# One emformer attention + ReGLU kernel: a new load order in the head, other block sizes, and a re-timed planner

## The chip, the cores and the metric

The kernel runs on one NeuronCore of a Trainium2 chip. The metric is the device time of one execution in microseconds (us). The core has a matrix engine (TensorE, PE in the profile, with its weight loads as PEld), a vector engine (VectorE, DVE), a scalar engine (ScalarE, ACT), GpSimd (POOL, which here mostly issues loads) and SyncE (SP, which here issues transfers). All transfers run on 16 DMA engines that these share.

## The reference

Two stages follow each other. The first is chunked attention: 4 batches, 8 heads, 768 positions, head size 64. Each chunk of 32 queries sees 8 memory keys, 16 keys to its left, its own 32 and 8 to its right.

```python
k_full = np.concatenate([mem_k, k_ctx], axis=2)
v_full = np.concatenate([mem_v, v_ctx], axis=2)
scores = scale * np.matmul(q_c, k_full.transpose(0, 1, 3, 2))
scores = scores - np.max(scores, axis=-1, keepdims=True)
a = np.exp(scores)
a = a / (np.sum(a, axis=-1, keepdims=True) + 1e-09)
out[:, :, c_start:c_end] = np.matmul(a, v_full)
```

The second is a gated feed-forward layer on the 3072 rows that result (512 wide, 1536 hidden):

```python
gate = np.maximum(x @ w_gate, 0.0)
val = x @ w_val
return (gate * val @ w_out).astype(np.float32)
```

## The kernel before

**Tiles and blocks.** The 3072 rows are 24 tiles of 128 rows, six to a batch. Attention runs tile by tile: `scores` (L297), `row_max` (L315), `subtract` (L325), `exponent` (L334), `row_sum` (L340), `reciprocal`, `normalise` (L348), a transposition of P, `values` (L369), and `x_copy` (L392), which puts the tile's attention output, already transposed, into a block's `xT`. The feed-forward layer runs block by block: a block is 2 to 4 consecutive tiles (`BLOCKS`, L51). `first` (L402) multiplies all of a block's columns by 128 hidden units of a gate or value weight, four matmuls to a group; `relu` (L411) on ACT and `gate` (L416) on DVE make the hidden activations; `second` (L428) makes the output rows and `store` (L436) copies and writes them. A block's `first` needs all of its tiles' `x_copy`. Blocks 0 and 1 (tiles 0 to 3) are interleaved by four weight groups (`GROUPS`: hidden pieces 0-1, 2-5, 6-8, 9-11), as the weights arrive.

**Batch 0 and the rest.** For tiles 0 to 5, q and k are loaded in pairs of tiles (`load_pair`, L226) and transposed on PE with an identity (`pair_t`, L234); ACT or DVE copies the result out of PSUM (`pair_copy`, L240). v of batch 0 is loaded in its natural layout (`load_v_tile`, L196) and shifted to the chunks' contexts on PE (`shift`, L205) and copied (`shift_copy`). For later tiles, q and k are loaded tile by tile (`load_qk`), and v of a batch is loaded straight into `v_bd`. From tile `LATE_QK` on, a transposing DMA issued by SP does the q and k transposition (`qk_transfer`, L281) in place of PE (`qk_t`, L275), and one copy of the keys remains; the scores read the queries where the DMA put them. From tile `LATE_P` on, SP also transposes P (`p_transfer`, L361) in place of PE and a copy (`p_t`, `p_copy`).

**Order of the work.** All instructions are emitted by a planner written in the kernel (`schedule`, L692). Each operation has the engines that may run it with planned durations, its dependencies, a priority, and buffers that it takes and gives back. The planner steps through planned time, gives each free engine its first ready operation by priority (attention of a tile comes before feed-forward work), and appends it to that engine's program. The engines then execute those programs in order, each waiting where its next operation's data are not there yet. So a planned duration moves no instruction by itself; it changes the order. Planned landings of loads are in L746-750; those of the SP transfers in L779-781 with `LAND` and `LAND_P` (L518-519) added. Until a planned 18 us (`WARM`), PE is given products on zeros (`idle_product`) wherever it has nothing ready.

**Queues.** POOL issues the loads in the order of the calls from L644 on. SP issues the small memory-value rows of batch 1 and the transposing DMAs. The load of v for batch 2 waits until `v_bd[0]` is cleared, which is planned after `("tc", 12, 1)`, the key copy of tile 12; the load of v for batch 3 waits for `hold` (L684), planned after the values of tile 11 and the key copy of tile 17. Loads of q and k of tile 16 and later stand behind v of batch 2 in POOL's order.

Of the kernel before, what the change touches and what calls it, by code (L numbers as in the profile page):

```python
# [19 lines left out]
def kernel(  # L20
# [29 lines left out]
    NSET = 2  # L50
    BLOCKS = [2, 2, 2, 4, 4, 4, 4, 2]  # L51
    GROUPS = [(0, 2), (2, 6), (6, 9), (9, 12)]
    BAND0 = 48
    UT = 3

    LATE_QK, LATE_P = 11, 10

# [459 lines left out]
    ISSUE, SLACK = 1.5, 1.0  # L517
    LAND = {a: 4.0 if a < 16 else 3.5 if a < 19 else 2.0 for a in range(NT)}  # L518
    LAND_P = {a: 3.0 if a < 14 else 2.5 if a < 18 else 2.0 for a in range(NT)}

# [3 lines left out]
    for a in range(NT):  # L524
        b, t = divmod(a, TPB)
        last = t == TPB - 1
        for i in (1, 0):
            if b == 0:
                if t % 2 == 0:
                    for j in range(2):  # L530
                        op(("t", a + j, i), {"PE": 0.3}, lambda e, a=a, i=i, j=j: pair_t(a // 2, i, j),
                           [("pl", a // 2, i), "ib", ("new", b)], (1, a - i, -2 + j), ["aps"], ["qk"] * j)
                        op(("tc", a + j, i), psum16(HP * 128) if t else {("ACT", "DVE")[j]: psum16(HP * 128)[("ACT", "DVE")[j]]}, lambda e, a=a, i=i, j=j: pair_copy(a // 2, i, j, engine[e]),
                           [("t", a + j, i)], (1, a - i, -2 + j), (), ["aps"])
# [125 lines left out]
    for par in range(2):  # L660
        load(("vm", par), 256, 0.3, lambda par=par: mem_values(par))
    for a, i in late[:5]:
        load_qk_op(a, i)
    for i in range(2):
        load(("wo", i), 768, 4.1, lambda i=i: load_out(i))
    for b in range(1, B):
        deps = ([("z0", hp, c0) for hp in range(HP) for c0 in range(0, NCH, 8)] if b > 1 else [("z1", hp) for hp in range(HP)]) + ([("v", TPB * (b - NSET + 1) - 1)] + ['hold'] if b > NSET else [])
        if b == 1:
            for n in range(2 * HP):
                op(("mr", b, n), {"SP": 0.72}, lambda e, b=b, n=n: mem_rows(nc.sync, b, n),  # L670
                   deps + [(("vm", 0), 0.2), (("vm", 1), 0.2)], (0,))
        for par in range(2):
            load_v_op(b, par, deps)
        if b == 2:
            for n in range(2 * HP):
                load(("mr", 2, n), 192, 0.22, lambda n=n: mem_rows(nc.gpsimd, 2, n),
                     deps + [(("vm", 0), 0.2), (("vm", 1), 0.2)])
        for a, i in late[(5, 20, 26)[b - 1]:(20, 26, 36)[b - 1]]:
            load_qk_op(a, i)
    for n in range(2 * HP):  # L680
        load(("mr", 3, n), 192, 0.22, lambda n=n: mem_rows(nc.gpsimd, 3, n),
             deps + [(("vm", 0), 0.2), (("vm", 1), 0.2)])

# [8 lines left out]
    def schedule():  # L692
        done, started, times = {}, set(), [0.7]
        free = {e: 0.7 for e in ("PE", "ACT", "DVE", "SP", "POOL")}
        queue_end, flying, gives = 0.0, [], [(WARM + 0.15, "fps")]
        room["fps"] -= 1
# [27 lines left out]
        while len(started) < len(ops) + len(loads):  # L724
# [8 lines left out]
            while moved:  # L733
                moved = False
                for e in ("POOL", "PE", "ACT", "DVE", "SP"):
                    if free[e] > t + 1e-9:
                        continue
                    if e == "POOL":
# [98 lines left out]
```

## Time and profile before

| what | value |
|---|---|
| median of 3 runs (lowest, highest) | 241.21 us (241.03, 241.58) |
| the profiled execution's own time | 240.65 us |
| its span, first to last instruction | 238.9 us |
| PE busy, of the span | 232.5 us, 97% |
| DVE, ACT, POOL busy | 145.3, 135.5, 77.4 us |
| mean granted TensorE clock | 0.998 of full speed |
| first feed-forward product starts | 22.89 us |
| last PE work ends | 235.1 us |

Times in the profile are microseconds from the start of the span. A row of the timeline gives start, length from first start to last end, engine, the kernel's line, operation, what it writes and reads, the shapes, how many instructions are merged in it, and in brackets how long the engine stood idle before and what ended that. Matmul ends are modelled and overlap with the next start, so that the time a group really takes is read from start to start.

### The profile page before, as it was taken

To read this page: it belongs to the slowest core of one execution; us is meant where nothing else is said; L and a number is where in the kernel's file an instruction comes from. 1 tells how busy PE (TensorE), PEld (TensorE's weight loads), DVE (VectorE), ACT (ScalarE), POOL (GpSimd) and SP (SyncE) were. 2 spreads that over 40 slices of the span, in tenths; PEclk is the share of its full clock that TensorE was granted. 3 is DMA by queue.
4 is the path that set the end of the run, shared out by engine and by line. 5 is a ranking of instruction groups with operands and counts; after the bars stand their busy time and mean duration, and the time that the engine had idled before them with its cause. 6 is when DMAs were issued, how large, how long until landed. Compare 5 with 4: busy or idle time off the path is not lost.

```text
span 238.9 us, 6437 instructions
## 1 busy us (share of the span) xinstructions
PE 232.5 (97%) x2654; PEld 137.7 (58%) x2654; DVE 145.3 (61%) x292; ACT 135.5 (57%) x284; POOL 77.4 (32%) x102
## 2 busy tenths in 40 slices
PE   7898999999999999999999999999999999999994
PEld 5577887785589644455544444444555444445873
DVE  6674876987888389994279851599960043410430
ACT  7577777866885456897566851365523233312422
POOL 8975779313920374700094552100000000000000
PEclk9999999999999999999999999999999999999999
DMA  6999999999999999996199999995121300012102
GB/s 74 171 179 202 201 166 161 206 133 125 190 166 138 131 156 118 122 129 136 70 141 101 135 154 91 113 209 64 27 43 47 127 4 0 0 47 88 44 3 88
DMA packets 103069, 26.88 MB, mean 113 GB/s; under 512 B 94080, under 2 KB 99968, under 8 KB 103040
## 3 DMA queue, kind: packets, MB, share of 16 engines
q0 software_dynamic: 76128, 14.65, 92.7%
q1 hardware_dynamic: 23312, 5.53, 23.2%
q10 hardware_dynamic: 3600, 6.29, 8.4%
q8 instruction: 21, 0.34, 0.7%
q14 instruction: 8, 0.07, 0.2%
HBM read 28.55 MB, written 6.29 MB: 146 GB/s over the span
## 4 chain that ended last, share of the span: by engine, by line
PE 93%; DMA 2%; POOL 2%; issue 1%; ACT 1%; ACTq 0%; POOLq 0%
PE v_ps L408 27%; PE g_ps L408 26%; PE out_ps L433 26%; PE xT_ps L389 3%; PE s_ps L310 2%; DMA v_n<-in_v_dram 2%; PE idle_ps L140 2%; PE vs_ps L216 2%; PE xT_ps L382 2%; PE qk_ps L279 1%; PE pT_ps L359 1%; POOL qk_p L229 1%; PE qk_ps L238 1%; PE xT_ps L375 1%; POOL v_n L200 0%
## 5 line engine op out<-in xcount | busy, mean ns | idle before, releaser
L420 DVE TENSOR_TENSOR gvT<-v_ps,g_relu 128x256 f16<-128x256 f32 (+1 forms) x96 | 53.0, 554 | 48.7 <-PE v_ps L408 35.1
L408 PE MATMUL v_ps<-xT,w_val_sb 128*128 128x256 f16 (+1 forms) x384 | 78.2, 326 | 0.1
L408 PE MATMUL g_ps<-xT,w_gate_sb 128*128 128x256 f16 (+1 forms) x384 | 78.1, 326 | 0.0
L414 ACT ACTIVATE g_relu<-g_ps 128x256 f16<-128x256 f32 (+1 forms) x96 | 47.0, 490 | 41.5 <-PE g_ps L408 39.8
L433 PE MATMUL out_ps<-w_out_sb,gvT 128*128 128x512 f16 (+2 forms) x300 | 65.8, 371 | 0.0
L408 PEld LDWEIGHTS <-w_gate_sb 128*128 128x128 f16 x384 | 36.9, 98 | 24.8
L408 PEld LDWEIGHTS <-w_val_sb 128*128 128x128 f16 x384 | 35.9, 98 | 22.5 <-issue 0.5
L433 PEld LDWEIGHTS <-gvT 128*128 128x128 f16 x300 | 27.6, 97 | 29.5
L79 ACT COPY o_sb<-out_ps 128x512 f32<-128x512 f32 (+2 forms) x25 | 14.2, 568 | 29.6 <-PE out_ps L433 19.4
L323 DVE TENSOR_REDUCE mx<-s_ps 128x8 f32<-128x512 f32 x24 | 16.4, 685 | 13.9 <-PE s_ps L310 13.5
L338 ACT ACTIVATE p_exp<-dif 128x256 f16<-128x256 f32 (+2 forms) x72 | 19.6, 339 | 6.3 <-DVE dif L330 6.1
L184 POOL DMA_DIRECT2D v_bd<-in_v_dram x12 | 11.0, 924 | 33.6 <-DVE v_bd L684 19.2
L342 DVE TENSOR_REDUCE sm<-p_exp 128x8 f32<-128x512 f16 x24 | 16.4, 683 | 5.0 <-ACT p_exp L338 4.8
L257 POOL DMA_DIRECT2D qk_b<-in_k_dram x18 | 16.2, 902 | 9.7 <-DMA v_bd<-in_v_dram 5.4
L257 POOL DMA_DIRECT2D qk_b<-in_q_dram x18 | 16.2, 899 | 9.7 <-DMA v_bd<-in_v_dram 7.2
L79 ACT COPY v_bd<-v_bd 24x768 f16<-24x768 f16 (+1 forms) x23 | 18.5, 823 | 1.2 <-ACT o_sb L79 0.9
L353 DVE TENSOR_TENSOR p_n<-p_exp,rinv 128x512 f16<-128x512 f16 x24 | 16.5, 686 | 0.3
L330 DVE TENSOR_TENSOR dif<-s_ps,mx 128x512 f32<-128x512 f32 x24 | 16.2, 674 | 0.2
L79 ACT CAST xT<-xT_ps 128x512 f16<-128x512 f32 x17 | 10.0, 586 | 8.5 <-PE xT_ps L389 7.3
L167 POOL DMA_DIRECT2D v_bd<-vmem x16 | 10.2, 645 | 12.4 <-DMA qk_b<-in_q_dram 6.1
L140 PE MATMUL idle_ps<-idle 128*128 128x256 bf16 x69 | 11.3, 314 | 1.1 <-DVE warm L477 1.1
L389 PEld LDWEIGHTS <-v_bd 128*128 128x128 f16 x288 | 9.8, 96 | 3.6
(60 smaller groups left out, 165.6 us busy)
## 6 DMA issues: line engine op xcount, KB each, us to landing
out_dram<-o_sb ACTq DMA_DIRECT2D x23, 256.0 KB
qk_b<-in_k_dram POOLq DMA_DIRECT2D x18, 128.0 KB, 8.0
qk_b<-in_q_dram POOLq DMA_DIRECT2D x18, 128.0 KB, 8.9
v_bd<-in_v_dram POOLq DMA_DIRECT2D x6, 384.0 KB, 11.2
w_out_sb<-in_moe_w_out_dram POOLq DMA_DIRECT2D x2, 768.0 KB, 10.5
qk_p<-in_k_dram POOLq DMA_DIRECT2D x3, 256.0 KB, 5.3
qk_p<-in_q_dram POOLq DMA_DIRECT2D x3, 256.0 KB, 6.3
v_n<-in_v_dram POOLq DMA_DIRECT2D x6, 128.0 KB, 6.5
```

The source lines that it names most:

```text
L79: nc.scalar.copy(o, i)
L257: nc.gpsimd.dma_start(qk_b[a][:, 1 - i], bass.AP(tensor=x.tensor, offset=x[b, 0, 128 * t, 0].offset, ap=[[D, 128], [S * D, H], [1, D]]))
L323: nc.vector.reduce_max(SM[a, "mx"], s4, axis=AX.X)
L330: nc.vector.tensor_tensor(out=SM[a, "dif"].rearrange("p (m r) a s -> p r m a s", r=2), in0=S_ps.pop(a).rearrange("p r (m a) s -> p r m a s ...
L338: nc.scalar.activation(p[:, :, :, s0:s0 + k1 - k0], dif[:, :, :, k0:k1], ACT.Exp, scale=SCALE)
L342: nc.vector.reduce_sum(SM[a, "sm"], SM[a, "p"], axis=AX.X)
L353: nc.vector.tensor_tensor(out=P_n[a], in0=SM.pop((a, "p")), in1=rinv_b, op=ALU.mult)
L389: nc.tensor.matmul(ps[:, hp, r], lhsT=v_bd[b % NSET][:, hp, 4 * t + g, :], rhs=x[:, hp, r], start=True, stop=True)
L408: nc.tensor.matmul(ps, lhsT=w[:, f, 128 * m:128 * m + 128], rhs=xTs[blk][:, f, :], start=(f == 0), stop=(f == NFC - 1))
L414: nc.scalar.activation(st["r", m], st.pop((0, m)), ACT.Relu)
L420: nc.vector.tensor_tensor(out=st["gv"][:, m, :], in0=st.pop((1, m)), in1=st.pop(("r", m)), op=ALU.mult)
L433: nc.tensor.matmul(st["o", t, c], lhsT=st["gv"][:, m, 128 * t:128 * t + 128], rhs=w_out_sb[:, m, c[0]:c[1]], start=(m == 0), stop=(m == ND ...
```

## The change

It has five parts.

1. **Load order in the head.** The second pair's q (tiles 2 and 3) is loaded after v of tiles 0 and 1, ahead of v of tile 2 and of the first weight group. It stood behind both.
2. **Keys ahead of exponents.** The transposition and copy of the second pair's keys get a priority right after the scores of tile 0, and the copies go to ACT. The first shift copies of v are planned after the exponent of tile 0 has begun, and the row sum of tile 0 after the subtraction of tile 1.
3. **Blocks.** 2, 2, 2, 3, 3, 4, 4, 2, 2 tiles in place of 2, 2, 2, 4, 4, 4, 4, 2.
4. **Transfers.** q and k are transposed by DMA from tile 10 on (before: 11), P from tile 9 on (before: 10).
5. **The planner's figures.** Other durations for the strided copies, other landing times for loads and for SP transfers (a model of turns in the queue), no factor of 1.8 on PE work in the first 8 us, and in the head DVE and ACT hold back any low-priority operation when a better one is planned within 0.45 us.

The order of the loads behind the head is now written as a list (`ORDER`); it is the same order as before.

```diff
-    BLOCKS = [2, 2, 2, 4, 4, 4, 4, 2]
+    BLOCKS = [2,2,2,3,3,4,4,2,2]
...
+    ORDER = [5, 'w0', 'w1', 'v1', 15, 'v2', 'm2', 6, 'v3', 10, 'm3']
+
+    LATE_QK, LATE_P = 10, 9
-
-    LATE_QK, LATE_P = 11, 10
...
+    STRIDED = {"ACT": (0.6, 0.75), "DVE": (0.66, 0.75)}
+    LAND = {a: 3.0 if a < 18 else 7.0 for a in range(NT)}
+    LAND_P = {a: 2.5 if a < 18 else 4.0 for a in range(NT)}
-    LAND = {a: 4.0 if a < 16 else 3.5 if a < 19 else 2.0 for a in range(NT)}
-    LAND_P = {a: 3.0 if a < 14 else 2.5 if a < 18 else 2.0 for a in range(NT)}
...
-                           [("pl", a // 2, i), "ib", ("new", b)], (1, a - i, -2 + j), ["aps"], ["qk"] * j)
+                           [("pl", a // 2, i), "ib", ("new", b)], (1, a - i, -2 + j) if (a, i) != (2, 1) else (1, 0, 1.5), ["aps"], ["qk"] * j)
...
-                           [("t", a + j, i)], (1, a - i, -2 + j), (), ["aps"])
+                           [("t", a + j, i)], (1, a - i, -2 + j) if (a, i) != (2, 1) else (1, 0, 1.5), (), ["aps"], [("s", 0)] if (a, i) == (2, 1) else [])
...
-        op(("sum", a), {"DVE": (0.6, 0.69)}, lambda e, a=a: row_sum(a), [("exp", a)], (1, a, 5), ["sm"])
+        op(("sum", a), {"DVE": (0.6, 0.69)}, lambda e, a=a: row_sum(a), [("exp", a)], (1, a, 5), ["sm"], (), [("sub", 1)] if a == 0 else [])
...
-                   (1, a, 7.6), (), ["fps"])
+                   (1, a, 7.6), (), ["fps"], [("exp", 0)] if t == 0 else [])
...
-    for t in range(3):
-        load_v_nat(t)
+    load_v_nat(0)
+    load_v_nat(1)
+    load_pair_op(1, 0)
+    load_v_nat(2)
     load_w_op(0)
-    load_pair_op(1, 0)
     load_pair_op(2, 1)
...
-                            done[key] = queue_end + (1.2 if n_load < 8 else 4.5 if key[:2] == ("vl", 1) else 2.4 if n_load < 45 else 6.0 if key[0] == "vl" else 4.0)
+                            done[key] = queue_end + (2.3 if n_load < 8 else 1.8 if key[0] == "w" else 4.5 if key[:2] == ("vl", 1) else 2.4 if n_load < 45 else 3.5 if key[0] == "vl" else 2.5)
...
-                                o = None if soon and key[0] in ("up", "z0") else ops[key]
+                                o = None if soon and (key[0] in ("up", "z0") or t < WARM + 4.0 and e in ("DVE", "ACT")) else ops[key]
                                 break
-                            soon = soon or ready(ops[key], t + 0.3)
+                            soon = soon or ready(ops[key], t + (0.45 if t < WARM + 4.0 else 0.3))
...
-                        d *= (1.8 if e == "PE" and t < 8.0 and key[0] in ("t", "p", "sh", "f") else 1.0)
...
                         if e == "SP" and key[0] in ("t", "pc"):
-                            queue_end = max(queue_end, t + 1.5) + {"t": 2.6, "pc": 1.3}[key[0]]
-                            done[key] = queue_end + 1.0
+                            double = key[0] == "t"
+                            busy = queue_end > t + 1.2
+                            begin = max(t + 1.2 + (3.0 if busy else 0.2), turn)
+                            if queue_end > begin:
+                                turn = begin + (3.8 if double else 2.7)
+                                queue_end += 1.6 if double else 0.9
+                            else:
+                                turn = begin + (1.5 if double else 0.9)
+                            done[key] = turn + 0.3
```

More of the change, by code (lines that the diff above doesn't have):

```diff
@@ L531 @@
                         op(("t", a + j, i), {"PE": 0.3}, lambda e, a=a, i=i, j=j: pair_t(a // 2, i, j),
-                           [("pl", a // 2, i), "ib", ("new", b)], (1, a - i, -2 + j), ["aps"], ["qk"] * j)
-                        op(("tc", a + j, i), psum16(HP * 128) if t else {("ACT", "DVE")[j]: psum16(HP * 128)[("ACT", "DVE")[j]]}, lambda e, a=a, i=i, j=j: pair_copy(a // 2, i, j, engine[e]),
-                           [("t", a + j, i)], (1, a - i, -2 + j), (), ["aps"])
+                           [("pl", a // 2, i), "ib", ("new", b)], (1, a - i, -2 + j) if (a, i) != (2, 1) else (1, 0, 1.5), ["aps"], ["qk"] * j)
+                        op(("tc", a + j, i), {"ACT": STRIDED["ACT"]} if (a, i) == (2, 1) else STRIDED if t else {("ACT", "DVE")[j]: STRIDED[("ACT", "DVE")[j]]}, lambda e, a=a, i=i, j=j: pair_copy(a // 2, i, j, engine[e]),
+                           [("t", a + j, i)], (1, a - i, -2 + j) if (a, i) != (2, 1) else (1, 0, 1.5), (), ["aps"], [("s", 0)] if (a, i) == (2, 1) else [])
                 continue
@@ L661, with v_deps, mem_deps @@
         load(("vm", par), 256, 0.3, lambda par=par: mem_values(par))
[L662 to L668, printed above, removed]
-            for n in range(2 * HP):
[L670 to L682, printed above, removed]
+    def v_deps(b):
+        z = [("z0", hp, c0) for hp in range(HP) for c0 in range(0, NCH, 8)] if b > 1 else [("z1", hp) for hp in range(HP)]
+        return z + ([("v", TPB * (b - NSET + 1) - 1), "hold"] if b > NSET else [])
+    def mem_deps(b):
+        return v_deps(b) + [(("vm", 0), 0.2), (("vm", 1), 0.2)]
+    n_qk = 0
+    for step in ORDER:
+        if isinstance(step, int):
+            for a, i in late[n_qk:n_qk + step]:
+                load_qk_op(a, i)
+            n_qk += step
+            continue
+        kind, b = step[0], int(step[1])
+        if kind == "w":
+            load(("wo", b), 768, 4.1, lambda b=b: load_out(b))
+        elif kind == "v":
+            for par in range(2):
+                load_v_op(b, par, v_deps(b))
+        else:
+            for n in range(2 * HP):
+                load(("mr", b, n), 192, 0.22, lambda b=b, n=n: mem_rows(nc.gpsimd, b, n), mem_deps(b))
+    if "m1" not in ORDER:
+        for n in range(2 * HP):
+            op(("mr", 1, n), {"SP": 0.72}, lambda e, n=n: mem_rows(nc.sync, 1, n), mem_deps(1), (0,))
     op("hold", {"DVE": 0.1}, lambda e: nc.vector.memset(v_bd[1][0:2 * CH, 0, 0, :].bitcast(F32), 0.0), [("v", 2 * TPB - 1)],
@@ L694, in schedule @@
         free = {e: 0.7 for e in ("PE", "ACT", "DVE", "SP", "POOL")}
-        queue_end, flying, gives = 0.0, [], [(WARM + 0.15, "fps")]
+        queue_end, turn, flying, gives = 0.0, 0.0, [], [(WARM + 0.15, "fps")]
         room["fps"] -= 1
@@ L779, in schedule @@
                         if e == "SP" and key[0] in ("t", "pc"):
-                            queue_end = max(queue_end, t + 1.5) + {"t": 2.6, "pc": 1.3}[key[0]]
-                            done[key] = queue_end + 1.0
+                            double = key[0] == "t"
[4 more added lines that the diff above has]
+                                queue_end += 1.6 if double else 0.9
+                            else:
+                                turn = begin + (1.5 if double else 0.9)
+                            done[key] = turn + 0.3
                         elif queue_end > t and key[0] == "oc":
```

## The prediction

> **What bounds the kernel now.** I read the busy totals first, then stretches of the head, then PE's timeline, then the landings of the loads.
>
> ```profile
> PE 232.5 (97%) x2654; PEld 137.7 (58%) x2654; DVE 145.3 (61%) x292; ACT 135.5 (57%) x284; POOL 77.4 (32%) x102
> ```
>
> PE is the bound, but "busy" includes products on zeros and modelled ends. So I went through PE's timeline from start to start. A group of four 256-column products advances it by 0.44 us (22.89 to 23.33), a group of four 512-column ones by 0.865 us. At such prices, from 24.5 us to the last product nothing is lost but some 0.6 us near 44. PE can finish sooner only by wasting less before 24.5 us, or by having less to do. The stretches of the head, with busy time and count for PE, PEld, DVE, ACT, POOL, then granted clock, share of DMA and GB/s:
>
> ```profile
> 12.00:18.00 6.00, 6.00 (x102) 4.75 (x101) 4.26 (x8) 4.41 (x12) 4.68 (x7) 1.00 1.86 179
> 18.00:24.00 6.00, 5.03 (x151) 4.29 (x152) 2.54 (x4) 4.39 (x9) 3.24 (x6) 1.00 1.31 203
> ```
>
> PE's timeline shows what that "6.00" is:
>
> ```profile
> 11.64 1.38 PE L140 MATMUL idle_ps<-idle 128*128 128x256 bf16 x11
> 12.95 0.31 PE L310 MATMUL s_ps<-kT,qT 64*32 64x64 bf16 x32
> 13.96 2.47 PE L140 MATMUL idle_ps<-idle 128*128 128x256 bf16 x21
> ...
> 17.02 0.41 PE L238 MATMUL qk_ps<-ident_b,qk_p 128*64 128x128 bf16 x8
> ...
> 19.27 0.41 PE L238 MATMUL qk_ps<-ident_b,qk_p 128*64 128x128 bf16 x8 [0.35 <-ACT xT L79]
> ...
> 19.94 0.68 PE L382 MATMUL xT_ps<-pT,v_bd 56*64 56x32 f16 x32
> ...
> 22.49 0.47 PE L238 MATMUL qk_ps<-ident_b,qk_p 128*64 128x128 bf16 x9 [0.63 <-issue]
> ```
>
> The zero products (L140) advance PE by 1.31, 2.31, 0.53 and 0.23 us, and two gaps cost 0.52 (18.75 to 19.27) and 0.70 (around 22): **5.6 us without useful work from 11.64 to 24.9 us**. The scores at 12.95 are tile 1's; tile 1's values start at 19.62; the first feed-forward group starts at 22.89. Tile 1's scores waited for a key copy that stands behind v copies on ACT, and the first exponent stands behind that copy:
>
> ```profile
> 12.00 0.74 ACT L79 COPY kT<-qk_ps 128x512 bf16<-128x512 bf16 x1
> 12.59 0.82 ACT L338 ACTIVATE p_exp<-dif 128x256 f16<-128x256 f32 x3
> ```
>
> **Load order.** The second pair's q (0.95 us of POOL, 256 KB) moves ahead of one v load (0.9 us) and four weight loads (2.5 us). It was issued at 10.00 and landed 6.3 us later, at 16.3; issued at 6.65 it lands at about 13, as loads of this stretch take 5.2 to 5.9 us. What it is moved past gets later by one load's share of the stream, 256 KB at 180 GB/s or 1.4 us: v of tile 2 from 12.6 to 14.0, the first weight group from 15.4 to 16.8. v of tile 2 feeds tile 1's shift (13.19), whose result is first read by tile 1's values (after 17); the weights are first read after 19. Both are hidden; without cover each costs up to 1.4 us. From the pair of tile 4's keys on, bytes and issues ahead are the same, so the second weight group still lands by about 24.9 us (second value load: issued at 15.5, some 9 us to landing). SP issues none of these.
>
> **Keys ahead of exponents.** Both copies on ACT follow tile 0's scores at 10.29 and, 0.6 us on, at 10.9; the second ends at 11.6 instead of 12.74. Next late is tile 0's subtraction, which frees the one score buffer at 11.27 + 0.69 = 11.96. So tile 1's scores start at 12.05 (0.9 earlier), tile 0's exponent at 12.0 (0.6 earlier). The v copies now queue behind that exponent on ACT, two of 0.6 us, to 13.9; their reader, tile 0's values, comes after 16. On DVE follow tile 1's maximum 12.5, its subtraction 13.1, tile 0's sum 13.7, reciprocal and normalisation 14.5; tile 1's exponent is done at 14.7, its sum 15.2, its normalisation 15.9 to 16.6 (before: 17.85). From there 0.25 PE, 0.45 copy, 0.95 values and 0.6 copy, plus waits of 0.1 to 0.2 between engines and half a microsecond behind q's copies, end tile 1's chain at 19.3 (before: 21.25). First feed-forward group: 19.4.
>
> What PE does in that time: from 11.64 to 19.4 there are 5.3 us of work (two scores 0.5, three shifts 1.2, two pairs of transpositions 1.4, two P 0.45, two values 1.85), so 2.5 are lost. From 19.4 to 24.9 I find 4.75 of 5.5 us: the first weight group of block 0 1.75, one gate group of the second 0.45, shifts of tiles 2 and 3 1.15, tile 2's P and values 1.15, tile 3's scores 0.25. The loss falls from 5.6 to 3.2 us; I add 0.4 back for one more gap of the kind seen twice. **Gain 2.0 us**, between 0 (PE fills with nothing) and 3.1 (no wait for weights). Not below 0: what waits longer (two loads, two v copies) has the slack given above.
>
> **Clock.** [...] The row at 18 to 24 us keeps 1.00 with 0.97 us idle in it; the last stretch, with 3.1 us idle, averages 0.95. [...] No row here shows half a clock. My 5.5 us hold only 0.75 idle, and I take no clock cost.
>
> **Blocks.** Two blocks of four tiles become two of three and one of two, so 768 first-layer products become 864. Columns are the same; what is added is fixed time. 4 x 0.109 for 256 columns against 0.865/4 = 0.216 for 512 gives 2 x 0.109 - 0.216 = 2 ns each, **+0.2 us** (0.1 to 0.35 by rounding of starts). 384 columns lie between the two rows. ACT gets 12 more ReLUs: 386 ns for 256 columns, 595 for 512, so 177 fixed, 2.1 us in all; DVE 12 more gates: 420 and 688, 152 fixed, 1.8 us. Both lie beside PE (57 and 61% busy; 0.39 + 0.42 in 0.87 us of a two-tile pair). No stall sits at a block's start now, so the partition itself gains nothing; it does move needs (rival 2).
>
> **Transfers.** Tile 10's eight transpositions leave PE: 42.08 to 42.53 for eight, 0.45 us. Tile 9's P: 27.12 to 27.35, 0.23 us. **-0.7 us** on PE; three PSUM copies go for one SBUF key copy. SP issues two more: at 1.2 to 1.9 us each and idle 27.6 us on loads, it has room. Tile 10's loads land at 62.5, before tile 11's transfer starts at 65.06, so the later transfers keep their place; bound from the spacing there: 0 to 3.5 us later. P of tile 9 stands among them; tiles 9 to 11 are one block, needed near 109, and tile 11's values ran at 103.66, so 5 us cover it. If that cover goes, the cost is one for one.
>
> **Planner figures.** They cost nothing themselves; they order. q of tile 16 was issued at 95.75 and landed at 100.9, yet SP took that tile at 104.93; shorter planned landings can only bring this forward. For tiles from 18 on the longer `LAND` puts key copies 3 to 4 us later, behind which scores and values of 18 and 19 queue. Bounds -0.3 to +1.0; I take **+0.3** for a late block start.
>
> **Sum.** The profiled execution took 240.65 (span 238.9, 1.75 around it): 240.65 - 2.0 + 0.2 - 0.7 + 0.3 = 238.45. It lies 0.56 below the median of the runs shown, 241.21, so the forecast for medians is **239.0**. The likeliest case's own range: 240.65 - 3.1 + 0.1 - 0.7 - 0.3 + 0.56 = 237.2 to, with half of the head's gain and of the late start's upper bound, 241.21 - 1.0 - 0.7 + 0.35 + 0.5 = 240.4.
>
> **Rival 1: weights bound the head.** If PE empties until 24.9 us, everything that is earlier just waits there. For it: 203 GB/s throughout 18 to 24, a full queue. Against: before, PE had a backlog of attention work at that point. Then only 0.2 - 0.7 + 0.3 remain: 241.0.
>
> **Rival 2, slower: block 5 waits for tile 15.** Tile 15 now belongs to a block (12 to 15) whose start moves ahead.
>
> ```profile
> 133.91 0.55 PE L389 MATMUL xT_ps<-pT,v_bd 128*128 128x32 f16 x16
> 134.87 0.69 DVE L81 CAST xT<-xT_ps 128x512 f16<-128x512 f32 x1
> ```
>
> That is tile 15, ready at 135.56. Ten tiles were through at 120.67; two more cost 2 x 7.87 (35.04 us between blocks 3 and 4, less 3.5 of attention, over 4), 0.65 of attention and 0.2, and less 0.7 and 2.0 the block could start at 134.6. At its old time tile 15 costs 1.0 us. It decides when tile 15 comes more than 2.0 us later than before: a wait of 3.0 undoes the gain of 2.5 and 0.5 more. Its chain hangs on tile 16's keys, loaded behind v of batch 2 (POOL waited there to 81.35). If tile 10's transfer pushes that by the whole 3.5 us, PE waits 4.5 and the time is 241.21 - 2.5 + 4.5 = 243.2. Against: the slack of four microseconds at SP named above.
>
> **Rival 3: the clock falls** in the head. If PE idles there for 3.1 us in one piece, as in the last stretch, and loses what that stretch did, 5% of 8.9 us, that is 3.1 - 0.75 + 0.45 = 2.8 on top: 241.8. [...] Against: the 1.00 at 18 to 24.
>
> **Chances.** About 0.2% (0.5 us) is what a measurement of this kernel can tell from no change. Forecast 0.60, all faster. Rival 1 0.15 (0.05 faster, 0.10 same). Rival 2 0.15, slower. Rival 3 0.03, slower. Order elsewhere that I can't place 0.07 (0.04, 0.01, 0.02). Faster 0.69, same 0.11, slower 0.20. The range of 237.0 to 241.9 leaves out most of rival 2 and a little below.
>
> **What would show it.** Right: tile 1's scores near 12.05, the second pair's q transposed by 14, fewer than 38 zero products after 11.6, the first feed-forward group near 19.4, no gap over 0.5 us behind 25, tile 10 gone from L279. Wrong: a first group after 21.4, PE idle up to 24.9, or a pause ahead of block 5 or 6 ended by an xT copy.

## The result: slower, and the profile after

The changed kernel takes 244.58 us in the median of four executions (243.64 to 251.62), the kernel before 241.13 beside it. The ratio is 1.0126, with a 95% interval of 1.0091 to 1.0162; of the four, the one at 251.62 is left out of it (what happens in such executions is the subject of one experiment below). A second set of five executions gave 1.0075 (1.0052 to 1.0097). So the change costs about 1%, some 2.4 us, where a gain of 2.2 us had been forecast.

The profiled execution took 243.64 us: span 241.9, 3.0 more than before. In it the kernel's lines are numbered one or two higher than before (L409 is `first`, L434 `second`). Busy totals of the page, after:

```profile
PE 234.0 (97%) x2733; PEld 145.9 (60%) x2733; DVE 146.7 (61%) x301; ACT 138.8 (57%) x297; POOL 78.0 (32%) x102
```

PE is the bound as before, at the same share. As before, only its timeline from start to start tells more. Stretches of the head after, with the columns of the table shown of before (busy time and count of PE, PEld, DVE, ACT, POOL, then granted clock, share of DMA, GB/s):

```profile
18.00:24.00 6.00, 4.96 (x107) 3.60 (x106) 4.24 (x8) 3.68 (x8) 3.04 (x5) 0.91 1.34 202
24.00:30.00 6.00, 6.00 (x110) 4.50 (x109) 4.24 (x8) 2.88 (x9) 4.08 (x6) 0.81 1.31 201
22.00:24.00 2.00, 1.51 (x12) 1.07 (x12) 1.12 (x3) 1.04 (x3) 0.61 (x1) 0.73 1.26 204
24.00:26.00 2.00, 2.00 (x43) 1.23 (x41) 0.58 (x2) 0.48 (x2) 1.11 (x2) 0.50 1.30 200
```

The clock column is new: both six-microsecond rows had 1.00 before. From 24 to 26 us PE ran at half its clock. PE's timeline of the head, after:

```profile
11.94 0.39 PE L141 MATMUL idle_ps<-idle 128*128 128x256 bf16 x2
12.27 0.31 PE L311 MATMUL s_ps<-kT,qT 64*32 64x64 bf16 x32
...
13.17 0.64 PE L239 MATMUL qk_ps<-ident_b,qk_p 128*64 128x128 bf16 x16
...
14.84 2.03 PE L141 MATMUL idle_ps<-idle 128*128 128x256 bf16 x17
16.71 0.39 PE L360 MATMUL pT_ps<-band,p_n 128*128 128x128 f16 x4
...
18.98 0.40 PE L360 MATMUL pT_ps<-band,p_n 128*128 128x128 f16 x4
...
20.83 0.41 PE L239 MATMUL qk_ps<-ident_b,qk_p 128*64 128x128 bf16 x8
21.69 0.27 PE L239 MATMUL qk_ps<-ident_b,qk_p 128*64 128x128 bf16 x3 [0.44 <-DVE xT L82]
22.49 0.33 PE L239 MATMUL qk_ps<-ident_b,qk_p 128*64 128x128 bf16 x5 [0.53 <-issue]
22.75 0.92 PE L409 MATMUL g_ps<-xT,w_gate_sb 128*128 128x256 f16 x4
23.47 1.06 PE L409 MATMUL v_ps<-xT,w_val_sb 128*128 128x256 f16 x4
24.32 1.06 PE L409 MATMUL g_ps<-xT,w_gate_sb 128*128 128x256 f16 x4
```

What was brought forward came forward: tile 1's scores stand at 12.27 (12.95 before), the second pair's q is transposed at 13.17. But tile 0's P is transposed at 16.71 behind 17 products on zeros, and the first feed-forward group starts at 22.75, where before it was 22.89. Its groups then take 0.72, 0.85 and 0.99 us each instead of 0.44. A third place lies far behind the head:

```profile
69.32 0.60 PE L409 MATMUL g_ps<-xT,w_gate_sb 128*128 128x256 f16 x4
69.76 0.56 PE L390 MATMUL xT_ps<-pT,v_bd 128*128 128x32 f16 x16
70.90 0.60 PE L409 MATMUL v_ps<-xT,w_val_sb 128*128 128x256 f16 x4 [0.58 <-ACT o_sb L80]
71.70 0.60 PE L409 MATMUL g_ps<-xT,w_gate_sb 128*128 128x256 f16 x4 [0.20 <-ACT g_relu L415]
```

PE pauses for ACT at 70 us; before, its rows show no pause in that stretch. Marks along the two traces: first output product 54.11 before, 55.44 after; block 2's first group 66.68 and 68.45; block 3's 85.47 and 87.26; last product's start 235.54 and 238.16; from there to the end of the span 3.34 and 3.69. (The 235.1 for the end of PE's work in the table of before is too early: its last product starts 0.4 us later.) Nearly two of the three microseconds are lost before block 2 starts.

### The profile page after: what moved, and what is told of

Read it like the earlier page. It is cut to its first block, busy times and chain, and to the rows that moved or that the text cites. A ratio compares the mean times of both kernels' runs of the same rounds, so it can differ in the third digit from the quotient of the medians.

```text
span 241.9 us, 6643 instructions
## 1 busy us (share of the span) xinstructions
PE 234.0 (97%) x2733; PEld 145.9 (60%) x2733; DVE 146.7 (61%) x301; ACT 138.8 (57%) x297; POOL 78.0 (32%) x102
## 4 chain that ended last, share of the span: by engine, by line
PE 81%; DMA 6%; ACT 5%; DVE 4%; issue 2%; POOL 1%; ACTq 1%; POOLq 0%
PE v_ps L409 24%; PE g_ps L409 24%; PE out_ps L434 21%; DMA v_bd<-in_v_dram 4%; PE xT_ps L390 2%; DMA qk_p<-in_k_dram 2%; PE s_ps L311 2%; PE idle_ps L141 2%; ACT v_bd L80 2%; PE vs_ps L217 1%; ACT p_exp L339 1%; PE xT_ps L383 1%; ACT o_sb L80 1%; PE qk_ps L239 1%; PE pT_ps L360 1%
## 5 line engine op out<-in xcount | busy, mean ns | idle before, releaser
L421 DVE TENSOR_TENSOR gvT<-v_ps,g_relu 128x256 f16<-128x256 f32 (+2 forms) x108 | 54.6, 508 | 66.5 <-PE v_ps L409 43.8
L409 PE MATMUL v_ps<-xT,w_val_sb 128*128 128x256 f16 (+2 forms) x432 | 80.7, 310 | 0.7 <-ACT o_sb L80 0.6
L409 PE MATMUL g_ps<-xT,w_gate_sb 128*128 128x256 f16 (+2 forms) x432 | 81.0, 311 | 0.2 <-ACT g_relu L415 0.2
L415 ACT ACTIVATE g_relu<-g_ps 128x256 f16<-128x256 f32 (+2 forms) x108 | 48.7, 454 | 48.2 <-PE g_ps L409 46.3
L434 PE MATMUL out_ps<-w_out_sb,gvT 128*128 128x512 f16 (+2 forms) x300 | 66.6, 371 | 0.0
L409 PEld LDWEIGHTS <-w_gate_sb 128*128 128x128 f16 x432 | 41.4, 98 | 21.0 <-issue 0.6
L409 PEld LDWEIGHTS <-w_val_sb 128*128 128x128 f16 x432 | 41.1, 98 | 20.4 <-issue 1.2
L434 PEld LDWEIGHTS <-gvT 128*128 128x128 f16 x300 | 27.7, 98 | 28.3
L80 ACT COPY v_bd<-v_bd 24x768 f16<-24x768 f16 (+1 forms) x25 | 20.0, 821 | 1.8 <-DMA qk_b<-in_q_dram 0.9
L185 POOL DMA_DIRECT2D v_bd<-in_v_dram x12 | 11.0, 933 | 28.6 <-ACT p_exp L339 20.5
L80 ACT CAST xT<-xT_ps 128x512 f16<-128x512 f32 x15 | 8.8, 585 | 8.0 <-PE xT_ps L390 7.2
L141 PE MATMUL idle_ps<-idle 128*128 128x256 bf16 x64 | 10.7, 317 | 1.1 <-DVE warm L478 1.1
```

The source lines that it names most:

```text
L80: nc.scalar.copy(o, i)
L141: nc.tensor.matmul(TMP["idle"][:, 0:N], lhsT=idle[:, 0:128], rhs=idle[:, 0:N], start=True, stop=True)
L409: nc.tensor.matmul(ps, lhsT=w[:, f, 128 * m:128 * m + 128], rhs=xTs[blk][:, f, :], start=(f == 0), stop=(f == NFC - 1))
L415: nc.scalar.activation(st["r", m], st.pop((0, m)), ACT.Relu)
L421: nc.vector.tensor_tensor(out=st["gv"][:, m, :], in0=st.pop((1, m)), in1=st.pop(("r", m)), op=ALU.mult)
L434: nc.tensor.matmul(st["o", t, c], lhsT=st["gv"][:, m, 128 * t:128 * t + 128], rhs=w_out_sb[:, m, c[0]:c[1]], start=(m == 0), stop=(m == ND ...
```

## Experiments

All ratios are to the kernel before on the same chip in the same set (its medians: 241.15, 240.97, 240.73 and 240.98 us in four sets).

**The changed kernel again.** No edit.

> The changed kernel once more, for a second trace and more times. In its first trace first-layer products between 22.75 and 26.5 us ran at a granted clock of 0.81 to 0.9, which cost about 1.2 us, and the first feed-forward group began at 22.75, no earlier than before. If the low clock belongs to the kernel (theory 1: too little PE work around 21 us), it is there again, in the same place, and the time is 243.5 to 245. If it was an accident of one execution (rival), the clock is 1.00 throughout, and the 3 us that are lost have to show elsewhere: pauses of PE behind 60 us.

242.48, 243.53 and 243.0 us, and two longer ones, 246.61 and 251.58; ratio 1.0075. The profiled execution (span 240.7) kept its clock:

```profile
18.00:24.00 6.00, 4.96 (x113) 3.70 (x112) 4.40 (x8) 3.52 (x8) 3.06 (x5) 1.00 1.35 201
24.00:30.00 6.00, 6.00 (x119) 4.96 (x118) 5.21 (x11) 3.64 (x10) 4.28 (x6) 1.00 1.31 201
```

The first group stood behind the same pauses (23.03 against 22.75), so the half clock is not fixed to the program. It can be priced: between 20 and 30 us PE's products take 1.5 us more beyond their usual length in the first execution than in this one, so **1.5 us, in some executions**. Without it the change still costs 0.75%.

### One part at a time

**The head alone** (load order, key priorities, the planner's figures for the head; old blocks, old transfers; the main lines of the edit):

```diff
-    for t in range(3):
-        load_v_nat(t)
-    load_w_op(0)
-    load_pair_op(1, 0)
+    load_v_nat(0)
+    load_v_nat(1)
+    load_pair_op(1, 0)
+    load_v_nat(2)
+    load_w_op(0)
...
+    (1, a - i, -2 + j) if (a, i) != (2, 1) else (1, 0, 1.5)
```

> The kernel before with the head alone changed: load order, key copies, their planned durations, the landing figures of the first eight loads and the weights, the holding back of DVE and ACT. Theory 1 (the head is where the loss arises: zero products keep PE from tile 0's P, and PE has too little work around 21 us): first group at 22.5 to 23, low clock behind it, 242 to 243.5 us. Rival (the head gains what I forecast, and the loss is in blocks or transfers): first group by 20.5, 239 to 240.

243.1 us, ratio 1.0069 (1.0028 to 1.0111). The part that was to gain 2.0 us costs 1.7. Its executions at a mean clock of 1.00 took 242.0 to 243.25, the two at 0.993 took 243.1 and 244.6.

**The blocks alone:**

```diff
-    BLOCKS = [2, 2, 2, 4, 4, 4, 4, 2]
+    BLOCKS = [2,2,2,3,3,4,4,2,2]
```

> The kernel before with the blocks 2,2,2,3,3,4,4,2,2 alone. By the prediction's term it costs 0.2 us of fixed time per product, 241.3. If a block's first product waits for its last tile (rival 2 of the prediction), 242.5 or more with a pause ahead of block 5 (tiles 12 to 15).

242.41 us, ratio 1.0046 (1.0031 to 1.0061): 1.1 us, all of it at a clock of 1.00. In its profiled execution (241.72, the quickest of five) the last product starts 0.66 us later than before, and 3.75 us instead of 3.34 lie behind it. Of the 0.66 the 96 products more explain 0.2 to 0.3. The pause near 21 us (last section) is 0.84 us instead of 0.63, and PE stands 0.25 us ahead of a tile's scores at 95.14, where before such a place costs 0.1. The longer end is not the blocks' own: the transfers alone, with the old blocks, have it too (3.69).

**The transfers alone** (old blocks):

```diff
-    LATE_QK, LATE_P = 11, 10
+    LATE_QK, LATE_P = 10, 9
...
-    LAND_P = {a: 3.0 if a < 14 else 2.5 if a < 18 else 2.0 for a in range(NT)}
+    LAND_P = {a: 2.5 if a < 18 else 4.0 for a in range(NT)}
```

with the new model of SP's queue and the new landing figures for late loads.

> The kernel before with transfers from tiles 10 and 9 and the new planned times of SP transfers and late loads alone. By the prediction's term PE has 0.7 us less to do: 240.5. If a late P or late keys hold PE (rival), pauses behind 60 us, as two of 0.74 and 0.36 us at 70 us in the changed kernel's trace, and 241 to 243.

251.5 to 256.4 us, ratio 1.0435 (1.0412 to 1.0459). With blocks of four, tile 9 belongs to block 3, which started at 85.47 before. PE's waits in this kernel:

```profile
89.60 0.40 PE L310 MATMUL s_ps<-kT,qk_T 64*32 64x64 bf16 x32 [2.69 <-DVE rinv L346]
96.44 0.42 PE L310 MATMUL s_ps<-kT,qk_T 64*32 64x64 bf16 x32 [6.44 <-DVE rinv L346]
97.67 0.59 PE L389 MATMUL xT_ps<-pT,v_bd 128*128 128x32 f16 x16 [0.81 <-DMA pT<-p_n]
99.66 1.87 PE L408 MATMUL g_ps<-xT,w_gate_sb 128*128 128x512 f16 x4 [1.40 <-DVE xT L81]
```

The rows put the waits of scores down to DVE. In the longest, DVE itself stands still behind ACT, and ACT behind a transfer of keys that SP issued at 85.28:

```profile
93.64 0.62 ACT L79 COPY kT<-qk_T 128x512 bf16<-128x512 bf16 x1 [5.70 <-DMA qk_T<-qk_b]
95.01 0.69 DVE L342 TENSOR_REDUCE sm<-p_exp 128x8 f32<-128x512 f16 x1 [4.12 <-ACT p_exp L338]
```

Block 3 starts at 99.66. With the new blocks the same transfers take 243 to 251 us (below), so it is the new blocks that make them bearable; the parts do not add up.

**Blocks and head, no new transfers** (the changed kernel with `LATE_QK, LATE_P = 11, 10` and the old figures for SP and late loads):

> The changed kernel with the transfers undone (q and k by DMA from tile 11, P from tile 10, and the old planned times of SP transfers and late loads); head and blocks as changed. If the transfers spare PE 0.7 us once tile 9 is not in block 3 (theory), this is slower than the changed kernel by about 0.7: 244. If they still cost, by the pauses of 0.7 and 0.4 us at 69 to 71 us and 0.3 at 92 and 98 (rival), those pauses are gone and it is 0.5 to 1 us quicker: 242.5 to 243.

242.54 to 243.21 us, ratio 1.0083 (1.0067 to 1.01). That is the changed kernel's time in its quicker executions (242.5 to 244.8). The transfers that take 0.7 us of products off PE bring nothing that can be seen. (The two sets ran on different chips, each beside the kernel before.)

**Blocks and transfers, the old head:**

> The changed kernel with the head undone; blocks and transfers as changed. If the head is what costs (theory 1: it brings PE nothing and lets the clock fall in many executions), this runs at 1.00 throughout and takes 241 to 241.8, with less spread than the changed kernel's 242.5 to 244.8. If blocks and transfers cost by themselves (rival), 242.5 or more.

243.12, 245.48, and two at 248.14 and 251.31 us; ratio 1.014 (1.0082 to 1.0198). The long executions come without the new head too, and none came without the new transfers: they come with the transfers.

### Inside the head

**The second pair's q held back** until tile 0's P is transposed:

```diff
 op(("t", a + j, i), {"PE": 0.3}, ..., ["aps"], ["qk"] * j
+   , [("p", 0)] if (a, i) == (2, 0) else []
```

> The changed kernel, with the transposition of the second pair's q planned behind tile 0's P in place of ahead of it. In the changed kernel tile 0's P starts at 16.71 us though its normalisation ends at 15.7. Theory: both transposition buffers in PSUM hold that q until ACT has copied it (15.43 to 16.77), so the planner puts P behind, with 17 zero products before it. Then P starts at 15.8 to 16.0 here and tile 1's P 0.4 to 0.8 us earlier than 18.98. Rival: the normalisation chain on DVE alone sets P's place, and P stays near 16.7. The time: within 0.5 us of the changed kernel's either way, as the first feed-forward group also waits for the keys of tile 4.

Tile 0's P moves from 16.71 to 16.16 and tile 1's from 18.98 to 18.42. So the early q does hold the two transposition buffers until ACT has copied it. But the first group stands at 23.02: behind tile 1's values PE has scores, shifts and 16 more transpositions first. The times, 245.79 to 251.79 with a ratio of 1.0275 (1.0189 to 1.0362), are those of the long waits that the transfers bring (below): its trace has one of 4.80 us for a transposed P at 123.69.

**Keys alone**, with the head's planner figures and the old load order:

> The kernel before with the keys ahead of exponents and the head's planned figures, but the old load order. If moving q's load ahead is what fills both transposition buffers and turns the head's gain into nothing, tile 0's P starts at 15.8 to 16 us here, 0.3 to 0.5 earlier than before, and the time is 240.8 to 241.4. If the keys and the figures cost by themselves, 242 or more.

241.54 to 241.91 us, ratio 1.0035 (1.0022 to 1.0048). Tile 0's P stands at 15.97, as expected when q does not fill the buffers, and still the first group comes at 23.08. PE pauses 0.77 us at 68.32 for ACT's copy of a q.

**Load order alone** (with the planner's landing figures of the head, and without the factor of 1.8):

> The kernel before with q's load moved ahead and the landing figures that go with it, but the keys in their old order. If moving the load is what costs, this is like the head alone, 242 to 244.6, with some executions at a low clock behind 22 us and the first feed-forward group at 23 or later. If it is the keys' order, 240.8 to 241.4.

243.36 us, ratio 1.011 (1.0081 to 1.0139). Yet the first output product comes at 52.80, **1.3 us earlier** than before. The trace shows the gain given back between 67 and 73 us, in pauses ahead of PE that ACT's or DVE's copies end:

```profile
68.83 0.38 PE L279 MATMUL qk_ps<-ident_b,qk_b 128*128 128x128 bf16 x4 [0.61 <-DVE pT L81]
```

and two more of 0.18 and 0.65, so that block 3 starts at 87.3 instead of 85.5.

**Products on zeros planned on** until the first group, up to a planned 22.5 us instead of 18:

```diff
-    WARM = 18.0
+    WARM, FILL = 18.0, 22.5
-                            if e == "PE" and 1.3 < t < WARM:
+                            if e == "PE" and 1.3 < t < FILL and (t < WARM or ("f", 0, 0, 0) not in started):
```

> The changed kernel with zero products planned on PE also between 18 and 22.5 us, until the first feed-forward group, wherever PE has nothing ready. Theory 1 (the clock falls because PE is too little busy between 20.8 and 22.7): fewer executions with a clock under 0.998, and a median nearer to the changed kernel's lowest times, 242.5. Rival (the fall has to do with other things than these gaps): medians as before, 243.5 to 244.6, with the clock at 0.99 in about half of the executions.

243.2 to 244.4 us and one of 252.35, ratio 1.0118: no better, and one of the ordinary executions is at 0.99 again. More zeros at this place cure nothing that can be measured.

### The long executions

The profile of that last kernel caught a long one. Its timeline of PE, then the chain that ended last, then what the lines of P's transfer (L364) and of the load of v (L185) did between 80 and 105 us, then stretches:

```profile
90.67 0.81 PE L409 MATMUL g_ps<-xT,w_gate_sb 128*128 128x384 f16 x4
99.81 0.59 PE L390 MATMUL xT_ps<-pT,v_bd 128*128 128x32 f16 x16 [8.32 <-DMA pT<-p_n]
```

```profile
87.85 11.91 DMA pT<-p_n
```

```profile
L364 SPq DMA_TRANSPOSE pT<-p_n x3: 1190/2164/2961, 87.8 to 96.4; - x3
...
L185 POOL DMA_DIRECT2D v_bd<-in_v_dram x4: 510/926/1332, 86.0 to 89.2; - x4
```

```profile
91.00:94.00 3.00, 0.49 (x3) 0.20 (x2) 0.57 (x1) 0.49 (x1) 1.20 (x2) 0.92 2.10 199
94.00:97.00 3.00, 0.00 (x0) 0.00 (x0) 1.82 (x4) 0.89 (x3) 0.00 (x0) 0.50 2.92 134
```

PE waits 8.32 us for tile 9's transposed P. The chain puts 11.91 us on that one transfer, issued at 87.85, behind a load of v for batch 2 that POOL had begun to issue at 86.0. The same lines of the changed kernel in its quick profiled execution:

```profile
L364 SPq DMA_TRANSPOSE pT<-p_n x4: 1192/1221/3017, 85.5 to 99.7; - x4
...
L185 POOL DMA_DIRECT2D v_bd<-in_v_dram x4: 520/930/1343, 86.9 to 90.1; - x4
```

Here P is ahead, at 85.49 against 86.9, and the values that read it run at 92.24 without a wait. The planner has the two issues 0.4 us apart, so that what happens in an execution decides their order. In the kernel before, the first transposed P was tile 10's, issued at 89.92 and read at 101.53: 11.6 us, where the changed kernel leaves 6.75. P ahead of the load was there within 6.75 us of its issue; P behind it took 11.91. What makes it so long behind the load no run separates.

Three more traces bear on it. In the long execution of blocks and transfers with the old head, POOL begins that load at 84.69; SP issues transposed keys at 86.65 and P at 87.97. P is read 16.6 us after its issue, and ACT stands at the copy of the keys, so that PE waits for a ReLU behind it:

```profile
95.13 0.62 ACT L79 COPY kT<-qk_T 128x512 bf16<-128x512 bf16 x1 [4.77 <-DMA qk_T<-qk_b]
```

```profile
96.19 0.81 PE L408 MATMUL v_ps<-xT,w_val_sb 128*128 128x384 f16 x4 [4.32 <-ACT g_relu L414]
104.58 0.55 PE L389 MATMUL xT_ps<-pT,v_bd 128*128 128x32 f16 x16 [2.35 <-DMA pT<-p_n]
```

In the transfers alone the load begins at 84.61, ahead of the keys of 85.28. So it is not P alone: transposed keys behind that load can hold PE too. Being behind is not always enough: with q held back, P of tile 9 was issued at 85.40, behind a load begun at 85.06, and PE waited 0.51 us for it; the 4.80 us there are for a P issued at 113.86, behind the load of v for batch 3 (from 112.54).

In the 8.32 us in which PE stood, the clock fell to 0.50 (the row of 94 to 97 us above). In the head 0.50 came after pauses of only 0.44 and 0.53 us, as PE was busy 4.96 of 6 us.

The test leaves both issues where they are and only plans the readers of tiles 9 to 11 about 6 us later:

```diff
-    LAND_P = {a: 2.5 if a < 18 else 4.0 for a in range(NT)}
+    LAND_P = {a: 9.0 if a < 12 else 2.5 if a < 18 else 4.0 for a in range(NT)}
```

> The changed kernel with one figure changed: the planned landing of P of tiles 9 to 11 is 9.0 us behind the transfer in place of 2.5, so the values of those tiles stand about 6 us later in PE's order. Theory: in part of its executions the changed kernel loses 8 us at 91 to 100 us, when the transfer of tile 9's P is issued behind the load of v of batch 2 instead of ahead of it and lands 12 us later (as in the trace of the kernel with more zero products: PE idle 8.32 us, ended by that transfer). Then no execution here is over 246 us, and the median is 242.5 to 243.5. Rival: the long executions come from the chip, whatever the kernel; then some of 250 us remain.

243.35, 244.41, 244.45 and 245.95 us, ratio 1.0155 (1.0104 to 1.0207). No execution is near 250. In its trace PE is busy all of 91 to 97 us; but there P was issued at 86.50, ahead of the load at 87.08.

**The same with the old head** (blocks, transfers, later readers):

> The kernel before with blocks, transfers and the same late values for tiles 9 to 11, head as before. If transfers spare PE 0.7 us (the prediction's term) and blocks cost what they do alone (241.7 to 242.4), this takes 241.2 to 241.8. If the transfers still cost elsewhere, 242.5 or more, with pauses of PE ended by a transposing transfer.

241.99 to 245.45 us, ratio 1.0104 (1.0042 to 1.0165), again none near 250; in its trace P is ahead as well (83.95 against 84.30). Eight executions none of which is over 246 us, against four at 248 or more among the thirteen of the same two kernels without this edit, support the reading and do not prove it: at four in thirteen, eight in a row without one come by chance in 5% of cases, and no trace shows P behind the load with a later reader. The later readers also cost a microsecond of their own: both traces have a pause that was not there, 1.09 us from start to start behind 115.37 and 1.19 behind 98.33.

### The order behind the head

The head's loss was still open. Each part of it costs something, and the places are 64 to 73 us, far behind anything that was edited. Either the planner's order there is worse, or the earlier work meets a limit that does not move. To tell these apart, every operation that the planner *of before* starts after a planned 30 us was kept on its engine and in its order; only the head is planned anew. The traces show that this was done: with 30 us, the groups of instructions on PE, ACT and DVE come in the order of before's trace from 28 to 32 us to the end.

```diff
+_FORCED = {"PE": [...], "ACT": [...], "DVE": [...], "SP": [...]}   # before's plan, from 30 us on
...
                         for _, key in todo[e]:
+                            if key in forced_set:
+                                continue
...
+                        if o is None and at[e] < len(_FORCED[e]) and not missing[_FORCED[e][at[e]]] and ready(ops[_FORCED[e][at[e]]], t):
+                            key = _FORCED[e][at[e]]
+                            o = ops[key]
+                            at[e] += 1
```

With the **load order alone**:

> Before with the second pair's q loaded ahead (with the head's landing figures), but every operation that the planner of before starts after a planned 30 us is kept on its engine and in its order of before. Theory A, the order behind the head gives the gain back: with the old order the pauses of 0.61, 0.18 and 0.65 us at 68 to 73 us are gone, and as the first output product of this load order came 1.3 us earlier (52.80 against 54.11), the time is 240.0 to 240.6, under before by some 0.3%. Theory B, the earlier work meets a limit that doesn't move (a landing, an engine that is full): PE pauses at another place between 50 and 90 us by as much, block 3 starts at 85.5 as before or later, and the time is 241.0 or more.

With the **keys alone**:

> Before with the keys copied ahead of the exponents and the head's planner figures, the old load order, and the order of before kept on every engine from a planned 30 us on. Theory A (order behind the head): the pause of 0.77 us near 68 us that this part showed without the fixed order is gone and the time is 240.6 to 241.2. Theory B: it is 241.5 again, as without the fixed order (241.61).

With the **whole head**:

> Before with the whole head of the change, and the order of before kept on every engine from a planned 30 us on. Theory A: the loss of 1.7 us that the head showed alone falls to what the granted clock takes; 241.0 or less where the clock stays at 1.00, the pauses of 0.30 and 0.23 us at 69 to 72 us gone. Theory B: 242.5 to 243.2 again.

With the load order alone, but the old order only **from a planned 40 us on**:

> As the first of this set, but the order of before is kept only from a planned 40 us on, so that the planner is free to put tile 3's values and block 1's first products earlier. Theory A: first output product at 53 or earlier, time 239.8 to 240.6. Theory B: 241.0 or more, with pauses between 50 and 90 us.

Ten executions of each, 31 of the kernel before:

| head, old order from | us | ratio (95%) | the same head, free order |
|---|---|---|---|
| load order, 30 us | 240.45 | 0.9971 (0.995 to 0.9992) | 1.011 |
| keys, 30 us | 241.05 | 0.9999 (0.9982 to 1.0015) | 1.0035 |
| whole head, 30 us | 240.61 | 0.998 (0.9961 to 1.0) | 1.0069 |
| load order, 40 us | 241.71 | 1.0022 (0.9999 to 1.0045) | 1.011 |

All three heads lose their cost, so the order was it: 0.4% to 1.4% by what the planner does behind 30 us. The pauses went with it: behind 25 us, the rows of the first three traces show no pause of PE over 0.15 us but one of 0.54 for a load. Already the stretch from 30 to 40 us, left free, costs half a per cent; its trace has a pause of 0.70 us from start to start behind 40.93. For the whole change, whose blocks and transfers rule out the old order, the same cause is inferred and not run. What the order did at 64 to 73 us can be read from ACT, in the head alone with the free order:

```profile
66.72 0.59 ACT L79 CAST xT<-xT_ps 128x512 f16<-128x512 f32 x1 [0.42 <-PE s_ps L310]
67.33 1.56 ACT L79 COPY v_bd<-v_bd 24x768 f16<-24x768 f16 x2
68.91 0.59 ACT L79 COPY pT<-pT_ps 128x512 f16<-128x512 f16 x1
69.52 0.81 ACT L338 ACTIVATE p_exp<-dif 128x256 f16<-128x256 f32 x3
...
71.22 0.38 ACT L414 ACTIVATE g_relu<-g_ps 128x256 f16<-128x256 f32 x1 [0.41 <-PE g_ps L408]
```

and in the same head with the old order:

```profile
67.48 0.57 ACT L80 COPY qT<-qk_ps 128x512 bf16<-128x512 bf16 x1
...
68.95 0.38 ACT L415 ACTIVATE g_relu<-g_ps 128x256 f16<-128x256 f32 x1 [0.42 <-PE v_ps L409]
69.23 0.58 ACT L80 COPY kT<-qk_ps 128x512 bf16<-128x512 bf16 x1
69.70 0.40 ACT L415 ACTIVATE g_relu<-g_ps 128x256 f16<-128x256 f32 x1
69.98 0.60 ACT L80 COPY pT<-pT_ps 128x512 f16<-128x512 f16 x1
```

In the first, two row copies of v (1.56 us) stand ahead of a copy of P, and PE waits for that copy ahead of the transpositions between block 2's first two groups, and then for one of q:

```profile
69.55 0.38 PE L279 MATMUL qk_ps<-ident_b,qk_b 128*128 128x128 bf16 x4 [0.30 <-ACT pT L79]
...
71.44 0.38 PE L279 MATMUL qk_ps<-ident_b,qk_b 128*128 128x128 bf16 x4 [0.23 <-DVE qT L81]
```

In the second the row copies are done by 66.8, and block 2's first group (67.22) is followed by no pause in the rows up to 75 us. (Its profiled execution, 241.44 us, is one of its slower ones; PE waits 0.54 us there for a load of keys at 61.49.) The table's first row is also the one version that is clearly quicker than both kernels, by 0.3% against the kernel before; the interval of the whole head ends at 1.0.

## Why the prediction was wrong

It forecast 239.0 us, with 237.0 to 241.9 and "faster" at 0.69; 244.58 lies above the range.

**"First feed-forward group: 19.4" and "Gain 2.0 us": the step that failed first.** The first starts came as worked out: tile 1's scores 12.27 (12.05 forecast), tile 0's exponent 11.95 (12.0). The normalisations came later by about half a microsecond: tile 0's 15.04 (from 14.5), tile 1's 16.60 to 17.29 (15.9 to 16.6). Then the sum added only durations of tile 1's chain, and "half a microsecond behind q's copies". In the trace tile 0's P waits until 16.71, as the early q fills both transposition buffers; tile 1's P stands at 18.98, the copy of its values ends at 21.63 instead of 19.3; and behind those values 16 transpositions of the third pair's keys (tiles 4 and 5) still stand before the first group. Holding q back gave 0.55 us of the P back and no earlier group, and neither did the keys alone, with tile 0's P at 15.97. The quantity to be forecast was PE's lost time, and it hardly fell: zero products, and what products take beyond their usual length, are 0.2 us less up to 30 us with the whole head and the old order behind it than before. That head is worth 0.2% (0.4 us by the medians, with an interval that reaches 0), not 2.0 us. The bound "between 0 and 3.1" held for the head itself.

**"Planner figures. They cost nothing themselves; they order": the step that was mis-sized.** The text bounded this from -0.3 to +1.0 and looked only at the transfers of tiles 16 to 19. The head's edits re-planned everything behind them, and that order costs 0.9% with the whole head (0.998 against 1.0069), about 2.1 us. Part of it is the granted clock: the three executions of the head alone at a clock of 1.00 have a median of 242.37, which leaves 0.7%. "Not below 0: what waits longer (two loads, two v copies) has the slack given above" was true of the four operations named and not of the program behind them.

**Blocks, "+0.2 us (0.1 to 0.35)".** Measured 1.1. The term counted the 96 products, which the trace bears out at 0.2 to 0.3; the longer end (+0.41), the longer pause near 21 us (+0.21) and the one ahead of scores (0.25) were not in it. Why the end is longer was not tried, and it comes with the old blocks too.

**Transfers, "-0.7 us on PE".** The products did go: 12 fewer transpositions of q, k and P for tiles from 6 on, at 56 ns each 0.7 us. In the quick executions nothing came of it. The condition "If that cover goes, the cost is one for one" was right, and the cover of 5 us was taken from the wrong place: it was read from tile 11's values in the old plan, but the new plan puts tile 9's values 6.75 us behind the issue of P. With the load of v in front, the transfer took 11.91 us and PE waited 8.32. Nor did the text price the transposed keys, which came late behind the same load in two traces (ACT waited 4.77 and 5.70 us for them). The load of v for batch 2 was in the text as a cause for rival 2 (tile 15) and not for tile 9.

**"I take no clock cost."** Rival 3, with 0.03, asked for 3.1 us of idle time in one piece. The clock fell to 0.50 with two pauses of 0.44 and 0.53 us, in some executions, at 1.5 us. Rival 3 counted 0.45 us for the clock itself (5% of 8.9 us) and named a condition that did not occur. What else decides it is open: the whole head with the old order has the same pauses (0.44 and 0.62) and PE busy 4.91 of the 6 us, and all ten of its executions stayed at 0.998 or more, though on another chip than those that showed 0.99. Two executions with the old head and the new transfers also read 0.992 and 0.993 (245.48 and 245.45 us); no trace shows where they lost it.

**Rivals 1 and 2** did not occur. Block 5 starts at 139.8 without a pause. In the changed kernel no row ahead of the first group waits for weights; what stands there is other PE work and two pauses, ended by a copy and by "issue".

Of the signs that would show it right, four held (scores of tile 1, q by 14, 28 zero products behind 11.6 us where before there were 38, tile 10 gone from PE's transpositions) and the two that carried the time failed (the first group, and no gap over 0.5 us behind 25).

## What to carry to other kernels

When a list scheduler plans the whole program, an edit to its first 20 us changes all the order behind them, and that can cost more than the edit gains; separate the two by keeping the old order behind the edit, which here turned +0.7% into -0.2%, and +1.1% into -0.3%. Forecast an engine's lost time, with the buffers that the moved work holds, rather than the start of one chain. Where two transfers are issued within half a microsecond of each other on different queues, price the reader for the worse order: here 8 us, in a part of the executions, the order of the two being the likeliest reason and not a proven one.

## What the hardware showed beside it

All eighteen traces have a pause of PE near 21 us, called "issue" in the rows, that stands behind 350 or 351 recorded products, whatever product comes next: 0.63 us before, 0.53 in both traces of the changed kernel, and this one in the load order with the old order behind it, inside tile 1's values:

```profile
21.05 0.65 PE L383 MATMUL xT_ps<-pT,v_bd 56*64 56x32 f16 x30
22.22 0.20 PE L383 MATMUL xT_ps<-pT,v_bd 56*64 56x32 f16 x2 [0.53 <-issue]
```

The operands of these 32 products had been there since the first of them. From start to start the pause took 0.4 to 1.6 us, so that it also moves the comparisons above by some tenths of a microsecond. A 16 KB transfer on a DMA queue that the profile calls "instruction" lies near 20 us each time. Whether the pause has to do with that transfer no run tested. For it: the three traces with the load order alone have one more such pause (0.46 us with the free order), 128 products earlier, at 15.75 to 16.15 us, and such a transfer lies ahead of that one as well, near 13 us. Against it: transfers of the same kind lie near 26 and 33 us, and no pause follows them.
